# Attention scores as sixteen small products in four quarters of TensorE's array, where four large ones with zero-padded keys stood

## The chip, the cores and the metric

The kernel runs on one core of one Trainium2 chip. The metric is the device time of one execution in microseconds, as the median of several runs. The engines are TensorE (PE; its weight loads are shown as PEld), VectorE (DVE), ScalarE (ACT), GpSimd (POOL) and SyncE (SP), whose queue issues nearly all transfers.

## The reference

Queries, keys and values have the shape (8 batches, 8 heads, 576 tokens, 64). Keys and values are averaged over groups of 8 tokens, so each query sees 72 of them. The attention's output, as a matrix of 4608 tokens by 512, goes through two dense layers with a softplus between.

```python
k_p = k.reshape(B, H, Sp, pool, D).mean(axis=3)        # Sp = 72, pool = 8
v_p = v.reshape(B, H, Sp, pool, D).mean(axis=3)
scores = scale * np.matmul(q, k_p.transpose(0, 1, 3, 2))
scores = scores - np.max(scores, axis=-1, keepdims=True)
attn = np.exp(scores)
attn = attn / (np.sum(attn, axis=-1, keepdims=True) + 1e-09)
attn_out = np.matmul(attn, v_p)
x = attn_out.transpose(0, 2, 1, 3).reshape(B * S, H * D)   # 4608 x 512
h = x @ w_in                                                # 512 x 2048
g = np.maximum(h, 0.0) + np.log1p(np.exp(-np.abs(h)))
out = g @ w_out                                             # 2048 x 512
```

## The kernel before, in words

The 4608 tokens are worked in 18 chunks of 256, each of two tiles of 128 tokens. A batch has 576 tokens, four and a half tiles, so 4 of the 36 tiles hold tokens of two batches: their first 64 tokens see one batch's keys and their last 64 the next one's.

For each tile, PE transposes the queries (`qTp`, L352), ACT copies them out of PSUM (`qT`, L359), PE makes the scores (`sc`, L365), and DVE takes the least of each head's 72 scores (`mn`, L373; the keys carry a negative factor, so the least stands for the greatest) and subtracts it (`E`, L381). In the first three chunks ACT takes the exponential straight from PSUM, with sums (L390). Later one ACT instruction exponentiates a whole chunk. After the sums come transposes of the probabilities (`ptp`, `ltp`), the products with the values (`avp`, L497), and the two dense layers: `h` (L516), the softplus on ACT, and `acc` (L539, L586) or, from chunk 6 on, seven products of quarters in Strassen's manner (`m`, L679), for which DVE forms sums (`sf`, `so`) and which DVE adds up at the end (`o`, `u`, L700). The dense layers use numbers split in a high and a low part, three products each.

The scores before the change: two heads lie one above the other in the 128 partitions of `qT` (64 each). `kbd` holds the scaled keys of such a pair in block form: the first head's 72 keys in partitions 0 to 63 and columns 0 to 71, the second's in partitions 64 to 127 and columns 72 to 143, and zeros elsewhere, which DVE writes once at the start (L180). ACT fills one block (L221) and DVE the other (L223), once per batch. A product of 128 by 128 queries with 144 columns gives two heads' scores of a tile. A tile takes four such products, two into each of two PSUM banks; each bank is a step of its own, with `least` and `less` behind it. A tile of two batches takes eight products, each for 64 tokens. A float32 product is two matmul instructions and two weight loads in the trace.

What sets the order. The program's two parts (the first three chunks with weights being prepared; then the steady part) are each written down as a list of operations with an engine, an estimated cost, predecessors and the buffers they need. A list planner (`Order.run`) plays them against these costs, and every engine's instructions are then issued in the order of its start times. So a changed cost or a merged step moves other instructions too. In the steady part two PSUM banks (kind "bank") serve the transposes, the scores and the value products; two serve `h`; four the outputs. SP's queue runs its transfers in the planned order and waits at each one for what it needs: query, key and value loads, the loads `w<-wi` (a ring for the first layer's weights, L707), and the stores `t<-t` (L654) and loads `w<-t` (L658) of the combined second-layer weights, prepared before chunk 6 by DVE and ACT (L641, L646, L650).

Of the kernel before, what the change touches and what calls it, by code (L numbers as in the profile page):

```python
# [9 lines left out]
F32 = mybir.dt.float32  # L10
# [84 lines left out]
def pooled_attention_softplus_ffn(  # L95
# [79 lines left out]
    kbd = [const.tile([P, HP, 2 * SP], F32, name=f"kbd{i}") for i in range(2)]  # L175
# [40 lines left out]
    def k_block(b, j, ps):  # L216

        pv = ps[j * D:(j + 1) * D, 0:HP * SP].rearrange("p (m j) -> p m j", m=HP)
        o = kbd[b % 2][j * D:(j + 1) * D, :, j * SP:(j + 1) * SP]
        if j == 0:  # L220
            nc.scalar.activation(out=o, in_=pv, func=AF.Copy, scale=SCALE)  # L221
        else:
            nc.vector.tensor_scalar(out=o, in0=pv, scalar1=SCALE, scalar2=None, op0=ALU.mult)  # L223

    def transpose_k(b, kp):
        ps = turn(at_banks, "kT")
        k_transposes(ps, kp)
        for j in range(2):
            k_block(b, j, ps)
# [111 lines left out]
    def new_E(c):  # L341
        e_[c] = one.tile([P, T, H, SP], F32, tag="E", name="E")

    class Tile:
# [16 lines left out]
        def scores(self, i, ps):  # L361
            for m in (2 * i, 2 * i + 1):
                for lo, hi, b in spans(self.first, self.first + P):
                    r = slice(lo - self.first, hi - self.first)
                    nc.tensor.matmul(out=ps[r, (m % 2) * 2 * SP:(m % 2 + 1) * 2 * SP],  # L365
                                     lhsT=self.q[:, m, r], rhs=kbd[b % 2][:, m, :],
                                     start=True, stop=True)

        def least(self, i, ps):

            if i == 0:
                self.mn = two.tile([P, H], F32, tag="mn", name="mn")
            nc.vector.tensor_reduce(out=self.mn[:, 4 * i:4 * i + 4], in_=self.view(ps), axis=AX.X,  # L373
                                    op=ALU.min)

        def view(self, ps):
            return ps[:, 0:4 * SP].rearrange("p (h j) -> p h j", h=4)

        def less(self, i, ps):
            hs = slice(4 * i, 4 * i + 4)  # L380
            nc.vector.tensor_tensor(out=e_[self.c][:, self.t, hs], in0=self.view(ps),  # L381
                                    in1=self.mn[:, hs].unsqueeze(2).to_broadcast([P, 4, SP]),
                                    op=ALU.subtract)

        def exp_sum(self, i, ps):
            if i == 0:
                self.sm = two.tile([P, H], F32, tag="sm", name="sm")
            for j in range(4):
                h = 4 * i + j
                nc.scalar.activation(out=e_[self.c][:, self.t, h], in_=self.view(ps)[:, j],  # L390
                                     func=AF.Exp, scale=-1.0, bias=self.mn[:, h:h + 1],
                                     accum_out=self.sm[:, h:h + 1])
# [62 lines left out]

    def att_tile(c, t):

        x = Tile(c, t)

        def qT():  # L460
            ps = turn(at_banks, "qTp")
            x.qT(ps)
            x.qT_out(ps)

        def scores():
            if c not in e_:
                new_E(c)
            for i in range(2):
                ps = turn(at_banks, "sc")
                x.scores(i, ps)  # L470
                x.least(i, ps)
                x.less(i, ps)

        def norm():
            x.sum()
            x.norm(nc.gpsimd)

        def PT():
            ps = turn(at_banks, "ptp")
            x.PT(ps)  # L480
            x.PT_high(ps)
            x.PT_low(ps)
            ps = turn(at_banks, "ltp")
            x.last(ps)
            x.last_high(ps)
            x.last_low(ps)

        return qT, scores, norm, PT
# [349 lines left out]
    def batch(b):  # L838
# [59 lines left out]
        for i in range(2):  # L898
# [21 lines left out]
        k_done[b] = [op(ACT, act(288), lambda: k_block(b, 0, s_t.tile), [o], [s_t]),  # L920
                     op(DVE, dve1(288) + 0.15, lambda: k_block(b, 1, s_t.tile), [o], [s_t])]
# [22 lines left out]
    def attend(c):  # L944
# [15 lines left out]
        for t, x in enumerate(tiles):  # L960
# [9 lines left out]
            ends = []  # L970
            for i in range(2):
                s = Slot("bank")
                p = op(PE, 0.55 * len(spans(x.first, x.first + P)),
                       lambda x=x, i=i, s=s: x.scores(i, bank(s, "sc")), [o, *keys], [s_qT, s])
# [127 lines left out]
    def keys_values(b):  # L1102
# [8 lines left out]
        for i in range(HP):  # L1111
# [7 lines left out]
        k_ready[b] = [op(ACT, act(288), lambda: k_block(b, 0, s_t.tile), [o], [s_t]),  # L1119
                      op(DVE, dve1(288) + 0.15, lambda: k_block(b, 1, s_t.tile), [o], [s_t])]  # L1120
# [17 lines left out]
    def steady_attention(c):  # L1138
# [10 lines left out]
        for x in tiles:  # L1149
# [6 lines left out]
            last = []  # L1156
            for i in range(2):
                s = Slot("bank")
                p = op(PE, 0.5 if len(sp) == 1 else 0.68,
                       lambda x=x, i=i, s=s: x.scores(i, bank(s, "sc")),  # L1160
# [209 lines left out]
```

## Time and profile before

| | us |
|---|---|
| median of 3 runs | 977.89 |
| the runs | 978.03, 977.89, 975.05 |
| the profiled execution, its own time | 975.02 |
| its span in the trace | 972.9 |
| PE busy in the span | 937.9 (96%) |
| DVE busy | 668.1 (69%) |
| ACT busy | 417.4 (43%) |

The span runs from the first to the last instruction of the trace; 2.1 us of the execution's time lie around it. PE's rows give each matmul a modelled end, so rows of neighbours overlap; what an instruction occupies is read from the starts of the one and the next.

### The profile page before, as it was taken

To read this page: it belongs to the slowest core of one execution; us is meant where nothing else is said; L and a number is where in the kernel's file an instruction comes from. 1 tells how busy PE (TensorE), PEld (TensorE's weight loads), DVE (VectorE), ACT (ScalarE), POOL (GpSimd) and SP (SyncE) were. 2 spreads that over 40 slices of the span, in tenths; PEclk is the share of its full clock that TensorE was granted. 3 is DMA by queue.
4 is the path that set the end of the run, shared out by engine and by line. 5 is a ranking of instruction groups with operands and counts; after the bars stand their busy time and mean duration, and the time that the engine had idled before them with its cause. 6 is when DMAs were issued, how large, how long until landed. Compare 5 with 4: busy or idle time off the path is not lost.

```text
span 972.9 us, 18364 instructions
## 1 busy us (share of the span) xinstructions
PE 937.9 (96%) x7232; PEld 892.0 (92%) x7232; DVE 668.1 (69%) x1468; ACT 417.4 (43%) x826; POOL 119.1 (12%) x149
## 2 busy tenths in 40 slices
PE   5889999999999999999999999999999999999998
PEld 4679898899888999999899999999999999999997
DVE  4799888433699853767788766676767666666654
ACT  4763333433444434435354435443435343444332
POOL 1000001015242100221332320023200000000000
PEclk9999999999999999999999999999999999999999
DMA  9845444133144778886686767487757564755562
GB/s 245 256 170 205 164 152 142 44 102 74 45 156 132 232 256 284 265 230 206 203 234 199 239 192 226 153 242 206 235 152 223 168 216 154 216 174 195 174 217 87
DMA packets 105382, 181.55 MB, mean 187 GB/s; under 512 B 45648, under 2 KB 59984, under 8 KB 105296
## 3 DMA queue, kind: packets, MB, share of 16 engines
q1 hardware_dynamic: 103216, 179.86, 60.0%
q8 instruction: 57, 0.93, 0.4%
q10 hardware_dynamic: 2080, 0.52, 0.3%
q14 instruction: 29, 0.24, 0.1%
HBM read 154.14 MB, written 26.21 MB: 185 GB/s over the span
## 4 chain that ended last, share of the span: by engine, by line
PE 81%; DVE 11%; ACT 4%; issue 2%; DMA 1%; DVEq 0%; ACTq 0%
PE h L516 37%; PE m L679 21%; PE acc L539 6%; PE acc L586 5%; PE sc L365 4%; PE avp L497 3%; DVE sf L605 2%; PE qTp L352 1%; PE ptp L427 1%; DVE d L641 1%; DVE so L615 1%; DVE gl L573 1%; DMA q<-in_q_dram 1%; DVE pm L405 1%; DVE o L700 1%
## 5 line engine op out<-in xcount | busy, mean ns | idle before, releaser
L516 PE MATMUL h<-xh,w 128*128 128x256 f32 x2304 | 421.5, 283 | 2.4 <-DVE w L813 1.2
L516 PEld LDWEIGHTS h<-xh,w 128*128 128x128 f32 x2304 | 355.9, 188 | 6.6 <-DVE w L813 1.7
L516 PE MATMUL h<-xl,w 128*128 128x256 f32 x1152 | 324.1, 281 | 0.0
L567 ACT ACTIVATE g<-h 128x512 f32<-128x512 f32 x240 | 130.5, 596 | 319.4 <-PE h L516 312.7
L516 PEld LDWEIGHTS h<-xl,w 128*128 128x128 f32 x1152 | 216.8, 188 | 0.0
L679 PE MATMUL m<-w,so 128*128 128x256 f32 x1152 | 152.9, 282 | 1.4 <-DVE o L700 1.4
L679 PEld LDWEIGHTS m<-w,so 128*128 128x128 f32 x1152 | 143.7, 188 | 1.8 <-DVE o L700 1.8
L605 DVE TENSOR_TENSOR sf<-g 128x128 f32<-128x128 f32 x192 | 58.5, 305 | 123.1 <-ACT g L567 122.8
L679 PE MATMUL m<-w,g 128*128 128x256 f32 x576 | 113.3, 286 | 0.0
L205 POOL TENSOR_TENSOR kst<-kst 72x512 f32<-72x512 f32 (+1 forms) x48 | 53.5, 1114 | 428.1 <-DMA kst<-in_k_dram 269.4
L573 DVE TENSOR_TENSOR gl<-g 128x512 fp32r<-128x512 f32 x120 | 86.0, 716 | 18.8 <-ACT g L567 18.7
L610 ACT CAST so<-sf 128x512 fp32r<-128x512 f32 x96 | 59.7, 622 | 65.7 <-DVE sf L605 64.5
L679 PEld LDWEIGHTS m<-w,g 128*128 128x128 f32 x576 | 87.9, 188 | 0.0
L679 PE MATMUL m<-w,gl 128*128 128x256 f32 x288 | 81.0, 281 | 0.0
L615 DVE TENSOR_TENSOR so<-sf,so 128x512 fp32r<-128x512 f32 x96 | 72.0, 750 | 7.6 <-ACT so L610 0.9
L373 DVE TENSOR_REDUCE mn<-sc 128x4 f32<-128x288 f32 x72 | 32.4, 455 | 44.0 <-PE sc L365 43.0
L586 PE MATMUL acc<-w,g 128*128 128x512 f32 x192 | 61.1, 399 | 0.0
L539 PE MATMUL acc<-w,g 128*128 128x512 f32 x192 | 60.6, 396 | 0.4 <-ACT g L522 0.4
L522 ACT ACTIVATE g<-h 128x256 fp32r<-128x256 f32 (+1 forms) x96 | 31.9, 383 | 57.8 <-PE h L516 45.8
L679 PEld LDWEIGHTS m<-w,gl 128*128 128x128 f32 x288 | 54.2, 188 | 0.1
L365 PE MATMUL sc<-kbd,qT 128*128 128x144 f32 (+1 forms) x320 | 47.0, 304 | 2.0 <-DVE kbd L223 1.0
L365 PEld LDWEIGHTS sc<-kbd,qT 128*128 128x128 f32 (+1 forms) x320 | 39.8, 187 | 7.5 <-ACT qT L359 3.1
(176 smaller groups left out, 1244.5 us busy)
## 6 DMA issues: line engine op xcount, KB each, us to landing
w<-wi SPq DMA_DIRECT2D x192, 512.0 KB
out_dram<-o SPq DMA_DIRECT2D x36, 256.0 KB
wst<-in_moe_w_in_dram SPq DMA_DIRECT2D x16, 512.0 KB
wst<-in_moe_w_out_dram SPq DMA_DIRECT2D x16, 512.0 KB
wi<-w SPq DMA_DIRECT2D x16, 512.0 KB
t<-t SPq DMA_DIRECT2D x16, 512.0 KB
w<-t SPq DMA_DIRECT2D x32, 256.0 KB
q<-in_q_dram SPq DMA_DIRECT2D x30, 256.0 KB
```

The source lines that it names most:

```text
L205: nc.gpsimd.tensor_tensor(out=out, in0=x, in1=y, op=ALU.add)
L365: nc.tensor.matmul(out=ps[r, (m % 2) * 2 * SP:(m % 2 + 1) * 2 * SP], lhsT=self.q[:, m, r], rhs=kbd[b % 2][:, m, :], start=True, stop=True)
L373: nc.vector.tensor_reduce(out=self.mn[:, 4 * i:4 * i + 4], in_=self.view(ps), axis=AX.X, op=ALU.min)
L516: nc.tensor.matmul(out=ps[:, 0:CT], lhsT=w[:, kc * P:(kc + 1) * P], rhs=x[:, kc], start=first and kc == j == 0, stop=last and kc == KC - 1 ...
L539: nc.tensor.matmul(out=accs[c][t], lhsT=a[:, ts], rhs=w, start=f == 0 and j == 0, stop=f == FC - 1 and j == 2)
L567: nc.scalar.activation(out=g, in_=ps.rearrange("p (k i) -> p k i", k=2), func=AF.Softplus)
L573: nc.vector.tensor_tensor(out=gl, in0=g, in1=gh.bitcast(F32), op=ALU.subtract)
L586: nc.tensor.matmul(out=accs[c][t], lhsT=a[:, k, ts], rhs=w, start=u == 0 and k == 0 and j == 0, stop=u == FP - 1 and k == 1 and j == 2)
L605: nc.vector.tensor_tensor(out=sf[:, o], in0=x, in1=y, op=how)
L610: nc.scalar.copy(out=so[:, 0], in_=ss[c, u])
L615: nc.vector.tensor_tensor(out=so[:, 1], in0=sf, in1=so[:, 0].bitcast(F32), op=ALU.subtract)
L679: nc.tensor.matmul(out=ms[c][n], lhsT=x, rhs=y, start=u == 0 and j == 0 and n in (1, 6, 5, 4), stop=u == FP - 1 and j == 2 and n in (2, 7, ...
```

## The change

The keys are kept without zeros. `kT` holds, for each pair of heads, the 72 scaled keys of the first head in partitions 0 to 63 and of the second in partitions 64 to 127; one ACT instruction writes it from PSUM, and DVE's instruction and the zeroing are gone. A tile's scores are now sixteen products: for each pair of heads `m`, each head `j` of it and each half `i` of the tile's 128 tokens, 64 partitions of queries (64 tokens) against 64 partitions of keys (72 columns). Head `j` picks the upper or lower half of the array's rows and also the PSUM bank; half `i` picks the left or right half of its columns and the upper or lower 64 partitions of the bank. So the four products that follow each other use four different quarters. A tile of two batches takes the same sixteen products, since its border lies at 64 tokens. All sixteen are one planned step that takes both banks at once. `least`, `less` and `exp_sum` then go by `j` (even heads, odd heads) where they went by halves of the heads; their sizes are the same, only the places in the output change.

The planner's cost for the step is 0.7 in place of two steps of 0.5 to 1.1 each, the chain of `least` steps changes slightly, and the stores `t<-t` get a higher priority (`first=1000`). An unused function is removed.

```diff
-    kbd = [const.tile([P, HP, 2 * SP], F32, name=f"kbd{i}") for i in range(2)]
+    kT = [const.tile([P, HP, SP], F32, name=f"kT{i}") for i in range(2)]
...
-        nc.vector.memset(kbd[i], 0.0)
...
-    def k_block(b, j, ps):
-
-        pv = ps[j * D:(j + 1) * D, 0:HP * SP].rearrange("p (m j) -> p m j", m=HP)
-        o = kbd[b % 2][j * D:(j + 1) * D, :, j * SP:(j + 1) * SP]
-        if j == 0:
-            nc.scalar.activation(out=o, in_=pv, func=AF.Copy, scale=SCALE)
-        else:
-            nc.vector.tensor_scalar(out=o, in0=pv, scalar1=SCALE, scalar2=None, op0=ALU.mult)
...
+    def k_scaled(b, ps):
+
+        nc.scalar.activation(out=kT[b % 2], in_=ps[:, 0:HP * SP].rearrange("p (m y) -> p m y", m=HP),
+                             func=AF.Copy, scale=SCALE)
...
-        def scores(self, i, ps):
-            for m in (2 * i, 2 * i + 1):
-                for lo, hi, b in spans(self.first, self.first + P):
-                    r = slice(lo - self.first, hi - self.first)
-                    nc.tensor.matmul(out=ps[r, (m % 2) * 2 * SP:(m % 2 + 1) * 2 * SP],
-                                     lhsT=self.q[:, m, r], rhs=kbd[b % 2][:, m, :],
-                                     start=True, stop=True)
+        def scores(self, pss):
+            for m in range(HP):
+                for j, ps in enumerate(pss):
+                    js = slice(j * D, (j + 1) * D)
+                    for i in range(2):
+                        r = slice(i * P // 2, (i + 1) * P // 2)
+                        b = (self.first + i * P // 2) // S
+                        nc.tensor.matmul(out=ps[r, m * SP:(m + 1) * SP], lhsT=self.q[js, m, r],
+                                         rhs=kT[b % 2][js, m], start=True, stop=True)
...
-        k_ready[b] = [op(ACT, act(288), lambda: k_block(b, 0, s_t.tile), [o], [s_t]),
-                      op(DVE, dve1(288) + 0.15, lambda: k_block(b, 1, s_t.tile), [o], [s_t])]
+        k_ready[b] = [op(ACT, act(288), lambda: k_scaled(b, s_t.tile), [o], [s_t])]
...
-            last = []
-            for i in range(2):
-                s = Slot("bank")
-                p = op(PE, 0.5 if len(sp) == 1 else 0.68,
-                       lambda x=x, i=i, s=s: x.scores(i, bank(s, "sc")),
-                       [o, *parts(sp, k_ready), *last], [s_qT, s], first=EARLY)
-                score_done[c].append(p)
-                last = [op(DVE, 0.46, lambda x=x, i=i, s=s: x.least(i, s.tile), [p], [s, s_mn])]
+            last, ss = [], [Slot("bank"), Slot("bank")]
+            p = op(PE, 0.7, lambda x=x, ss=ss: x.scores([bank(s, "sc") for s in ss]),
+                   [o, *parts(sp, k_ready)], [s_qT, *ss], first=EARLY)
+            score_done[c].append(p)
+            for i, s in enumerate(ss):
+                last = [op(DVE, 0.46, lambda x=x, i=i, s=s: x.least(i, s.tile), [p, *last],
+                           [s, s_mn])]
...
-                o = op(SYNC, 2.0, lambda u=u, part=part: put_t(u, part), [o], [s], lag=2.4)
+                o = op(SYNC, 2.0, lambda u=u, part=part: put_t(u, part), [o], [s], lag=2.4,
+                       first=1000)
```

How the instructions move, at the place where the scores of chunk 8 stand (417 us in the trace), between the last `m` products of chunk 6 and the first `h` products of chunk 7. PE's order before (`w` and `kbd` carry buffer numbers; a row of `sc` or `qTp` counts float32 products; most rows of `h` and `m` between are left out):

```order
L679 MATMUL m<-w_1413,gl 128x256
L352 MATMUL qTp<-ident,q 128x128 x8
L365 MATMUL sc<-kbd_98,qT 128x144 x4
L516 MATMUL h<-xh,w_1510 128x256 x2
...
L516 MATMUL h<-xl,w_1609 128x256
L365 MATMUL sc<-kbd_98,qT 128x144 x4
L516 MATMUL h<-xh,w_1510 128x256 x2
...
L212 MATMUL kT<-ident,kp 128x72 x4
L679 MATMUL m<-w_1704,g 128x256 x2
```

PE's order now, at the same place:

```order
L639 MATMUL m<-w_1477,gl 128x256
L341 MATMUL qTp<-ident,q 128x128 x8
L476 MATMUL h<-xh,w_1574 128x256 x2
...
L476 MATMUL h<-xl,w_1673 128x256
L361 MATMUL sc<-kT_98,qT 64x72 x16
L476 MATMUL h<-xh,w_1574 128x256 x2
...
L639 MATMUL m<-w_1177,so 128x256 x6
L361 MATMUL sc<-kT_98,qT 64x72 x16
L639 MATMUL m<-w_1768,so 128x256 x3
```

Twelve `h` instructions now stand between the query transposes and the first scores, and twelve `h` and twelve `m` (where only twelve `h` stood) between the scores of the first tile and those of the second. On DVE, before, at that place:

```order
L504 TENSOR_TENSOR xl<-avp,xh 128x512 x2
L373 TENSOR_REDUCE mn<-sc 128x4 x2
L381 TENSOR_TENSOR E<-sc,mn 128x288 x2
L373 TENSOR_REDUCE mn<-sc 128x4 x2
L381 TENSOR_TENSOR E<-sc,mn 128x288 x2
L223 TENSOR_SCALAR kbd_97<-kT 64x4x72
L605 TENSOR_TENSOR sf<-g 128x128
```

And now:

```order
L464 TENSOR_TENSOR xl<-avp,xh 128x512 x2
L368 TENSOR_REDUCE mn<-sc 128x4 x2
L374 TENSOR_TENSOR E<-sc,mn 128x4x72 x2
L565 TENSOR_TENSOR sf<-g 128x128
...
L660 TENSOR_TENSOR o<-o,m 128x256 x3
L368 TENSOR_REDUCE mn<-sc 128x4
L565 TENSOR_TENSOR sf<-sf,g 128x128
...
L368 TENSOR_REDUCE mn<-sc 128x4
L374 TENSOR_TENSOR E<-sc,mn 128x4x72 x2
```

The first tile's four instructions still follow each other, but those of the second come later, with sums of chunk 7 and the final additions of chunk 6 ahead of them and among them.

More of the change, by code (lines that the diff above doesn't have):

```diff
@@ L369, in least @@
[L369 to L374, printed above, removed]
-        def view(self, ps):
[L377 to L383, printed above, removed]
@@ new lines, in least, with less @@
+        def least(self, j, ps):
+            if j == 0:
+                self.mn = two.tile([P, 2, HP], F32, tag="mn", name="mn")
+            nc.vector.tensor_reduce(out=self.mn[:, j], in_=self.view(ps), axis=AX.X, op=ALU.min)
+        def view(self, ps):
+            return ps[:, 0:HP * SP].rearrange("p (m y) -> p m y", m=HP)
+        def less(self, j, ps):
+            nc.vector.tensor_tensor(
+                out=e_[self.c][:, self.t].rearrange("p (m j) y -> p j m y", j=2)[:, j],
+                in0=self.view(ps), in1=self.mn[:, j].unsqueeze(2).to_broadcast([P, HP, SP]),
+                op=ALU.subtract)
```

56 lines of the change are left out of this document (11 added, 45 removed).

## The prediction, as it was made

> **What bounds the kernel now.** I read the page first: its busy rows, its slices and the engine shares of the chain that ended last. Then came a table of windows (columns: window, its length, busy us of PE, PEld, DVE, ACT, POOL, then clock, DMA share, GB/s).
>
> ```profile
> PE 937.9 (96%) x7232; PEld 892.0 (92%) x7232; DVE 668.1 (69%) x1468; ACT 417.4 (43%) x826; POOL 119.1 (12%) x149
> PE   5889999999999999999999999999999999999998
> DVE  4799888433699853767788766676767666666654
> PE 81%; DVE 11%; ACT 4%; issue 2%; DMA 1%; DVEq 0%; ACTq 0%
> 0.00:25.00 25.00, 15.24 (x77) 11.06 (x78) 12.36 (x24) 10.58 (x42) 4.22 (x23) 1.00 0.97 244
> 50.00:100.00 50.00, 46.27 (x309) 41.33 (x308) 47.06 (x78) 24.40 (x60) 0.00 (x0) 1.00 0.56 196
> 520.00:700.00 180.00, 176.71 (x1484) 174.37 (x1484) 127.91 (x296) 79.87 (x134) 38.54 (x41) 1.00 0.72 214
> ```
>
> The reader is to see two regimes. From about 70 us on PE is never idle for long (176.71 of 180 us), while DVE has a quarter to spare: a microsecond taken from PE there shortens the run by a microsecond. Before that PE waits for loads, ACT and DVE, and only what lies on the chain counts. Of the 36 tiles, 6 (three chunks) are scored in the first 45 us; 30 are scored later, 27 of one batch and 3 of two (chunks 6, 11 and 15).
>
> **What a tile costs PE now.** Products by shape, all of the run (in the trace a float32 product is two instructions, so 256 instructions are 128 products); then PE's weight loads in order of time around one plain tile, and around the first half of a two-batch tile.
>
> ```profile
> L365 PE MATMUL sc<-kbd,qT 128*128 128x144 f32 x256 | 41.7, 304 | 1.5 <-DVE kbd L223 1.0 <-ACT qT L359 0.2
> L365 PE MATMUL sc<-kbd,qT 128*64 128x144 f32 x64 | 5.9, 305 | 0.5 <-ACT qT L359 0.5
> L365 PEld LDWEIGHTS sc<-kbd,qT 128*128 128x128 f32 x256 | 36.1, 198 | 5.4 <-ACT qT L359 2.1 <-DVE kbd L223 1.2 <-issue 0.8
> L365 PEld LDWEIGHTS sc<-kbd,qT 128*64 128x64 f32 x64 | 3.7, 141 | 2.1 <-ACT qT L359 0.9 <-issue 0.4 <-ACT xh L500 0.2
> 877.07 0.19 PEld L516 LDWEIGHTS h<-xl,w 128*128 128x128 f32 x1
> 877.19 1.04 PEld L365 LDWEIGHTS sc<-kbd,qT 128*128 128x128 f32 x8
> 878.17 0.31 PEld L516 LDWEIGHTS h<-xh,w 128*128 128x128 f32 x2
> 304.84 0.19 PEld L516 LDWEIGHTS h<-xl,w 128*128 128x128 f32 x1
> 305.16 0.44 PEld L365 LDWEIGHTS sc<-kbd,qT 128*64 128x64 f32 x8
> 305.80 0.54 PEld L365 LDWEIGHTS sc<-kbd,qT 128*128 128x128 f32 x4 [0.20 <-issue]
> ```
>
> Plain tile: loads start at 877.19, the next work's at 878.17, and the load before came 0.12 earlier, as usual. So eight instructions take 0.98 us, 0.1225 each: 144 columns.
>
> The two-batch half is the nearest thing to the change. Its eight instructions use 64 of the array's columns each, in turn the left and the right half. From 304.84 to 305.80 is 0.96 us; less the ordinary step of 0.12 it takes 0.84. Eight in a row at 0.1225 would be 0.98, and there is a pause of 0.20 behind (the bracket) and one as long ahead (305.16 less 304.84 less 0.12). What is left, 0.44, fits four steps of 0.1225 (0.49), not eight. So a left and a right half do run at once, and going into the halved array and out again costs 0.84 less 0.49 = 0.35 us. A two-batch tile has two such halves: 1.68 us.
>
> **The change, part by part.**
>
> *Scores.* A tile becomes 32 instructions of 72 columns, four to a group in four different quarters. If all four run at once, a group lasts as long as one: half the columns, half the time, 0.061 us. Its weight load does not bound it: the rows above differ by 57 ns between 128 and 64 columns (198 less 141), so 64 columns cost about 57 ns, just under 61. Eight groups are 0.49; one entry and one exit add 0.35: 0.84 us per tile. Bounds, since no row shows the array cut in rows as well as columns: below, 0.49 (no pause at all); above, 32 instructions with none at once, 1.95 + 0.35 = 2.30. I take 0.84, since the only split seen here overlaps fully. Gain: 27 × (0.98 − 0.84) = 3.8 us, and 3 × (1.68 − 0.84) = 2.5 us.
>
> The trace gives no instruction pace below a pair per 0.1225, so 61 ns per start; the change wants 15. The Trainium skill (TensorE: Matmul & The Clock Gate, "Wait — 56ns, not 53.3ns?") says that start-to-start never drops below about 25 ns however few the columns. By that a group would take 100 ns, a tile 0.80 + 0.35 = 1.15, and the scores' gain would turn into a loss of 3.0 us (27 × 0.17 lost, 3 × 0.53 gained). The pair row here neither confirms nor refutes it, as its mean of 61 ns lies above.
>
> *The wait for the copied queries.* In half of the later chunks the scores stood right behind the query transposes, and PE waited for ACT's copy (columns: us in total, times, longest).
>
> ```profile
> PEld sc L365 <- ACT qT L359: 3.1, 9, 0.5
> 417.04 1.14 PEld L365 LDWEIGHTS sc<-kbd,qT 128*128 128x128 f32 x8 [0.31 <-ACT qT L359]
> 430.38 2.84 PE h L516 x24
> 427.89 2.49 PE m L679 x21
> 875.60 0.95 DVE L373 TENSOR_REDUCE mn<-sc 128x4 f32<-128x288 f32 x2 [1.77 <-PE sc L365]
> 876.46 0.81 DVE L381 TENSOR_TENSOR E<-sc,mn 128x288 f32<-128x288 f32 x2
> DVE mn L373 <- PE sc L365: 43.0, 32, 4.0
> PE m L679 <- DVE o L700: 1.4, 2, 0.7
> ```
>
> Now twelve `h` instructions, half of 2.84 = 1.42 us, stand between, which covers both copies of the two tiles. Gain 3.1 us, of which I count 2.7, since one chunk has the key transposes (which need a bank that ACT frees) there first.
>
> *Both banks at once.* With two banks in all, the second tile's scores wait until DVE has done `mn` and `E` of the first on both: 0.95 + 0.81 = 1.76 us behind the end of the first scores. PE has 1.42 (`h`) + 12/21 × 2.49 = 1.42 (`m`), 2.84 us of other work, and DVE holds these four instructions right behind each other, already standing there (it waited 43.0 us in all for scores). Cost 0 with a cover of 1.1 us; without the cover, each chunk would stall up to 1.76. Queued behind a late `mn` are DVE's sums for `m` and `gl`. Before, the cover was 1.42 and the second tile showed no wait either. The second tile's `mn` and `E` come later now, behind the final additions (`o`), for which PE waited 1.4 us in all; by PE's order nothing needs those banks for two more `h` blocks. I allow −0.5 to +3 us, and take +1.0 for new small stalls of the moved order.
>
> *Keys.* DVE loses 8 instructions and two memsets; ACT's now covers 128 partitions with the same 288 columns, hence the same time.
>
> ```profile
> L223 DVE TENSOR_SCALAR kbd<-kT x8: 460/460/461, 16.0 to 705.5; 64x288 f32<-64x288 f32 x8
> 15.55 0.41 ACT kbd L221
> 15.99 0.47 DVE kbd L223
> 16.50 4.21 PE sc L365 x16
> 26.39 1.18 PE sc L365 x8
> 36.16 0.46 DVE kbd L223
> ```
>
> The last five rows are pieces of the chain of waits in the first 70 us. Two DVE pieces leave it, 0.93 us. The 16 first instructions took 4.21 us, 0.26 each, twice the later pace; four quarters at that pace give 2 × 2 × 0.84 = 3.4, so 0.8 less. Together 1.7, but loads share that stretch (DMA share 0.97) and the order of the first 70 us is mixed anew: bounds −3 (later) to +4 (sooner); I count 1.3 gained. The six later DVE instructions lie off the chain beside PE's work: 0.
>
> *Stores `t<-t`.* They move forward in SP's queue.
>
> ```profile
> SPq L654 <- DVE t L650: 28.2, 7, 8.9
> SPq L707 <- PE h L516: 399.3, 187, 9.5
> ```
>
> SP already stands waiting for DVE at seven of them. What queues behind are loads of later weights, which themselves wait for PE to free their buffers (399.3 us in all), so they hold slack; PE's waits name no such load. 0, and if a load came late, up to the longest wait of 8.9 us once.
>
> **Sum.** 3.8 + 2.5 + 2.7 + 1.3 − 1.0 = 9.3 us less. The profiled execution took 975.0 us (span 972.9 and 2.1 around it), so 965.7 on its own terms. It is at the bottom of the three runs shown, whose median is 2.9 higher; I put the changed kernel's median at 967.
>
> **Rivals.**
>
> 1. *Only two at once (the slower side).* If upper and lower halves of the array's rows take turns, a group takes 0.1225 and a tile 0.98 + 0.35 = 1.33 us. For it: every pair of 64-column instructions in this trace is left against right, none upper against lower. Against it: the quarters share neither partitions of input nor bank. It decides from 0.98, where a plain tile breaks even, which is a group of 0.079. Scores: 27 × 0.35 = 9.5 lost, 3 × 0.35 = 1.1 gained; with the other terms (2.7 + 1.3 − 1.0) 5.4 us slower, about 982 in the median's terms.
>
> 2. *Starts too slow.* Four run at once but cannot be started so fast; halfway between 61 and 122 ns a group takes 92, a tile 1.09. Scores: 27 × 0.11 = 3.0 lost, 1.8 gained; total 1.8 us faster, 975. By the Trainium skill's 25 ns, cited above, the whole change would come to nothing, 976. No overlap at all would be 27 × 1.32 + 3 × 0.62 − 3.0 = 34.5 us slower, 1011.
>
> 3. *New stalls.* The pairing of banks makes PE wait in each of the 14 steady chunks. For it: waits for DVE of up to 2.5 us exist at the probabilities' transposes. Against it: 1.1 us of cover. At 0.7 us each the gain shrinks by 10: no change, 977.
>
> **How the numbers follow.** The forecast 0.66; rival 1 0.11; rival 2 0.10 (without overlap 0.03 of it); rival 3 0.13. The forecast's own range is 959 to 972: the scores' lower bound 0.49 would bring 30 × 0.35 = 10 more, the start's +4 or −3. To hold 8 in 10 I reach up through rivals 2 and 3: 957 to 979. What this kernel's measurement tells from no change is about 0.3%, 2.9 us, so faster is below 975.0: the forecast, half of rival 2's likelier part and a good half of rival 3 make 0.75; slower (rival 1, no overlap, a little of 3) 0.15; the same 0.10.
>
> **What would show it.** In the changed trace the scores' weight loads come in fours at nearly the same time, the fours 0.06 us apart, with a pause of some 0.2 us on either side, and a tile takes 0.84 us from the load ahead to the load behind (rival 1: 1.33, rival 2: 1.09). The row of PE's scores waiting for `qT` is nearly gone; rows of `sc` waiting for DVE's `E` stay under 2 us in all (rival 3: 10). DVE has 10 instructions fewer of `kbd`. The forecast is wrong if a tile takes more than 0.98 us, or if the sum of PE's waits after 100 us grows by more than the scores give back.

## The result and the profile after

The changed kernel takes 961.52 us in the median of 4 runs (958.47 to 962.19), against 976.47 in 4 runs of the kernel before (973.75 to 978.03): a ratio of 0.984, with a 95% interval from 0.981 to 0.988. That is 15 us less; the forecast was a median of 967, range 957 to 979. A second series of the same kernel (below, as a run of its own) gave 959.6 and the same ratio. The profiled executions took 962.13 and 975.02, their spans 960.4 and 972.9.

First the page of the changed kernel, its busy rows and its chain by engine, then a table of windows (window, length, busy us of PE, PEld, DVE, ACT, POOL; clock, DMA share, GB/s).

```profile
PE 925.1 (96%) x8064; PEld 877.0 (91%) x8064; DVE 668.1 (70%) x1458; ACT 414.0 (43%) x824; POOL 120.2 (13%) x149
PE 83%; DVE 11%; ACT 3%; issue 2%; DMA 1%; DVEq 0%; ACTq 0%
```

```profile
0.00:25.00 25.00, 15.15 (x190) 10.50 (x191) 11.48 (x22) 11.33 (x42) 4.21 (x23) 1.00 1.06 253
50.00:100.00 50.00, 46.35 (x297) 41.93 (x296) 45.93 (x71) 19.75 (x46) 0.00 (x0) 0.97 0.53 190
520.00:700.00 180.00, 176.42 (x1637) 173.75 (x1636) 134.02 (x305) 80.71 (x136) 37.07 (x41) 1.00 0.70 217
```

PE's share is still 96%: the same engine bounds the kernel, with 12.8 us less to do (937.9 before). DVE has ten instructions fewer, and its busy time has not moved: two zeroings and eight key copies went, so what stayed takes as much longer.

The scores, as groups by shape, and PE's weight loads around one plain tile late in the run:

```profile
L361 PE MATMUL sc<-kT,qT 64*64 64x72 f32 x1152 | 26.7, 234 | 2.5 <-ACT kT L217 1.8 <-ACT qT L348 0.8
L361 PEld LDWEIGHTS sc<-kT,qT 64*64 64x64 f32 x1152 | 21.7, 138 | 8.6 <-issue 2.2 <-ACT kT L217 2.1 <-ACT qT L348 1.0
```

```profile
866.97 0.78 PEld L639 LDWEIGHTS m<-w,so 128*128 128x128 f32 x6
867.89 0.58 PEld L361 LDWEIGHTS sc<-kT,qT 64*64 64x64 f32 x32
868.55 0.53 PEld L639 LDWEIGHTS m<-w,so 128*128 128x128 f32 x4
```

There are 32 instructions where eight stood. The last of the six loads ahead started at 867.56, one ordinary step of 0.12 later would be 867.68, and the next work loads at 868.55: the tile takes 0.87 us. The single starts of the loads in the trace read 867.886, .893, .900, .906, then 867.941 to .961, 868.003 to .023, 868.066 to .086 and so on to 868.336: four within 20 ns, the fours 62 ns apart (55 for the first step). The products behind them start in the same fours, 7 ns apart: 868.001, .008, .015, .021. Of the 0.87, 0.21 is lost on the way into the quarters, about 0.15 on the way out, and 0.51 is work.

PE's waits after 100 us (total, times, longest) and, last, DVE's for the scores:

```profile
PE ptp L421 <- DVE pm L399: 4.1, 4, 1.3
PE qTp L341 <- DVE xl L464: 3.6, 4, 1.4
PEld sc L361 <- issue: 2.2, 6, 0.4
DVE mn L368 <- PE sc L361: 45.4, 16, 5.9
```

The row of the scores waiting for ACT's copied queries, 3.1 us before, is gone from this stretch, and so is the one of `m` waiting for `o`. The transposes' waits for DVE's `pm` and `xl` changed places (`ptp` for `pm` 2.7 before, for `xl` 2.8 before and 0.4 now; `qTp` 1.8 before) and are 8.1 us in sum, 7.3 before. All in all PE stood idle 13.2 us behind its 151st `h` instruction (92.2 us into the span), against 14.2 before (from 94.7).

Pieces of the chain of waits, in the start:

```profile
15.35 0.42 ACT kT L217
15.81 2.21 PE sc L361 x64
56.68 2.66 PE h L476 x12
61.30 1.44 PE h L476 x12
```

The keys are one piece, and the first two tiles' scores take 2.21 us, not 4.21. Their fours start 0.12 us apart, twice the later step, as the eight instructions of a tile did before (0.24 against 0.12). The trace's record of the clock begins only at 19.5 us (22.6 before), so the clock of 1.00 in the first window says nothing of them. The last two rows are a thing that the prediction did not ask about: the same twelve instructions took 2.66 us and then 1.44. The windows of that stretch, and the same window in the second series' profile of the same kernel, tell why:

```profile
54.40:57.00 2.60, 0.43 (x3) 0.32 (x3) 2.56 (x5) 0.66 (x2) 0.00 (x0) 1.00 0.10 41
57.00:60.40 3.40, 3.40 (x15) 3.13 (x14) 3.10 (x7) 0.66 (x2) 0.00 (x0) 0.51 0.31 123
```

```profile
57.00:60.40 3.40, 3.40 (x25) 3.15 (x24) 3.30 (x7) 0.66 (x2) 0.00 (x0) 1.00 0.27 107
```

PE had waited 2.17 us, and for the next 3.41 us the granted clock was half: 15 products instead of 25. In the other execution the wait was the same and the clock stayed whole. Such a stretch costs some 1.7 us: PE reached its 151st `h` instruction at 92.2 us in the one and at 90.5 in the other.

What differs is where the wait lies against a fixed step. In each of the 14 traces all recorded changes of the clock lie whole multiples of 3.413 us apart, within 3 ns. In the changed kernel's profile one such step runs from 53.63 to 57.04 us and holds the whole wait. In the second series' profile a border of steps, at 55.81, cuts the wait into 1.43 and 0.74 us (first row: the changed kernel's profile; then two of the second series'):

```profile
53.63:57.04 3.41, 1.24 (x11) 1.03 (x10) 3.37 (x7) 0.94 (x4) 0.00 (x0) 1.00 0.10 38
```

```profile
52.40:55.81 3.41, 1.99 (x17) 1.67 (x14) 3.37 (x6) 2.05 (x6) 0.00 (x0) 1.00 0.34 138
55.81:59.22 3.41, 2.67 (x17) 2.47 (x18) 3.27 (x8) 0.66 (x2) 0.00 (x0) 1.00 0.38 154
```

Over all traces, each of the 20 steps at full clock in which PE was busy for less than 0.49 of the time was followed by a half-clock step, none of those with more than 0.71 was, and of 107 in between 12 were (PE's busy time has modelled ends, so these shares are rough). One long wait is not needed: in the kernel before with its stores early (below), two waits, 0.53 and 0.47 us, lie in the step up to 254.66 us, and the next two steps have half the clock.

Each execution lists its mean granted clock, so **time lost to the clock** can be estimated for every run as its time times one less the clock. It leaves out the start, ahead of the clock's first record, and counts 0 to 1.2 us (by profile) at the very end, where the clock is recorded as half and PE is done. Among runs of one kernel, 0.76 us (± 0.10, one standard error, 135 runs) come with each us so lost: a little under one, perhaps as part of it falls where PE waits anyway. The table has means over a kernel's runs; "rest" is the mean less the loss.

| kernel | runs | mean us | lost to the clock | rest |
|---|---|---|---|---|
| before | 53 | 975.7 | 4.7 | 971.0 |
| before, stores early | 11 | 975.5 | 4.7 | 970.8 |
| before, both key blocks by ACT | 11 | 979.9 | 8.8 | 971.1 |
| old products as one step | 10 | 972.1 | 5.4 | 966.7 |
| new products, keys by two engines | 6 | 967.5 | 6.5 | 961.1 |
| the changed order, keys by two engines | 5 | 965.4 | 6.4 | 959.0 |
| changed (both series) | 10 | 960.4 | 2.0 | 958.3 |
| changed, score step planned at 0.87 | 4 | 959.4 | 2.4 | 957.0 |
| changed, DVE planned slower too | 5 | 964.8 | 5.6 | 959.2 |
| changed, stores as before | 10 | 974.3 | 7.8 | 966.5 |
| changed, left against right | 6 | 971.5 | 5.0 | 966.5 |
| changed, upper against lower | 4 | 968.1 | 0.5 | 967.7 |

The single runs of one kernel scatter by 0.9 to 2.3 us (one standard deviation) in "rest", so a mean of five is good to about 1 us. Of the change's 15.3 us, 12.7 are rest and 2.6 are clock.

### The profile page after: what moved, and what is told of

Same layout as the page of the kernel before. It is cut to its first block, busy times and chain, and to the rows that moved or that the text cites. A ratio compares the mean times of both kernels' runs of the same rounds, so it can differ in the third digit from the quotient of the medians.

```text
span 960.4 us, 20024 instructions
## 1 busy us (share of the span) xinstructions
PE 925.1 (96%) x8064; PEld 877.0 (91%) x8064; DVE 668.1 (70%) x1458; ACT 414.0 (43%) x824; POOL 120.2 (13%) x149
## 4 chain that ended last, share of the span: by engine, by line
PE 83%; DVE 11%; ACT 3%; issue 2%; DMA 1%; DVEq 0%; ACTq 0%
PE h L476 39%; PE m L639 22%; PE acc L499 7%; PE acc L546 6%; PE avp L457 4%; PE sc L361 2%; DVE sf L565 2%; PE qTp L341 2%; PE ptp L421 1%; DVE gl L533 1%; DVE so L575 1%; DMA q<-in_q_dram 1%; DVE d L601 1%; ACT g L527 1%; DVE pm L399 1%
## 5 line engine op out<-in xcount | busy, mean ns | idle before, releaser
L639 PE MATMUL m<-w,so 128*128 128x256 f32 x1152 | 155.0, 282 | 0.0
L204 POOL TENSOR_TENSOR kst<-kst 72x512 f32<-72x512 f32 (+1 forms) x48 | 51.3, 1069 | 463.3 <-DMA kst<-in_k_dram 223.0
L533 DVE TENSOR_TENSOR gl<-g 128x512 fp32r<-128x512 f32 x120 | 90.6, 755 | 24.5 <-ACT g L527 24.5
L482 ACT ACTIVATE g<-h 128x256 fp32r<-128x256 f32 x96 | 31.8, 382 | 60.8 <-PE h L476 46.6
L499 PEld LDWEIGHTS acc<-w,g 128*128 128x128 f32 x192 | 34.9, 191 | 7.5 <-ACT g L482 1.1
L546 PEld LDWEIGHTS acc<-w,g 128*128 128x128 f32 x192 | 34.4, 189 | 6.6
```

The lines of the kernel that those rows point to most:

```text
L204: nc.gpsimd.tensor_tensor(out=out, in0=x, in1=y, op=ALU.add)
L482: nc.scalar.activation(out=g, in_=ps[:, 0:CT], func=AF.Softplus)
L499: nc.tensor.matmul(out=accs[c][t], lhsT=a[:, ts], rhs=w, start=f == 0 and j == 0, stop=f == FC - 1 and j == 2)
L533: nc.vector.tensor_tensor(out=gl, in0=g, in1=gh.bitcast(F32), op=ALU.subtract)
L546: nc.tensor.matmul(out=accs[c][t], lhsT=a[:, k, ts], rhs=w, start=u == 0 and k == 0 and j == 0, stop=u == FP - 1 and k == 1 and j == 2)
L639: nc.tensor.matmul(out=ms[c][n], lhsT=x, rhs=y, start=u == 0 and j == 0 and n in (1, 6, 5, 4), stop=u == FP - 1 and j == 2 and n in (2, 7, ...
```

## The experiments

### Which quarters run at once

Three kernels issue a tile's sixteen products in other orders and are otherwise the changed one: pairs of left and right (head by head), pairs of upper and lower (token half by token half), and each quarter's eight instructions in a row. Their loops, in this order:

```diff
-            for m in range(HP):
-                for j, ps in enumerate(pss):
+            for j, ps in enumerate(pss):
+                for m in range(HP):
                     for i in range(2):
```

```diff
-            for m in range(HP):
-                for j, ps in enumerate(pss):
-                    for i in range(2):
+            for i in range(2):
+                for m in range(HP):
+                    for j, ps in enumerate(pss):
```

```diff
-            for m in range(HP):
-                for j, ps in enumerate(pss):
-                    for i in range(2):
+            for j, ps in enumerate(pss):
+                for i in range(2):
+                    for m in range(HP):
```

> The same sixteen products per tile, in another order: neighbours differ only in the left or right half of the array's columns, so only two quarters can be busy at once. Every engine's order is otherwise that of the changed kernel. Theory (the gain of the scores comes from four quarters at once): a pair every 0.0625 us, a tile 16 x 0.0625 + 0.37 = 1.37 us in place of 0.87, thus 30 x 0.50 = 15 us more than the changed kernel's 961.5, and 1 to 3 more at the start: 977 to 980. Rival (the gain comes from the moved order of the other instructions, the products hardly count): within 4 us of 961.5.

> The same sixteen products, neighbours differing only in the upper or lower half of the array's rows (and so in the bank). Theory (rows overlap as columns do): as left against right, 977 to 980, a pair every 0.0625 us. Rival (upper and lower halves overlap only when the columns differ too): one product after the other, a tile 32 x 0.0625 + 0.37 = 2.37 us, 45 us more: 1004 to 1010.

> The same sixteen products, four of one quarter in a row before the next quarter. Theory: nothing overlaps except where the quarter changes, a tile 2.2 to 2.4 us, 40 to 46 us more than the changed kernel: 1001 to 1012. Rival (products of a later quarter are pulled ahead of those that wait): close to 962.

Measured: left against right 971.06 us (ratio to before 0.995, 0.992 to 0.997), upper against lower 967.76 (0.991, 0.988 to 0.995), one quarter after the other 998.71 in one run. PE's weight loads around a tile in each, in this order:

```profile
874.42 0.78 PEld L639 LDWEIGHTS m<-w,so 128*128 128x128 f32 x6
875.34 0.88 PEld L361 LDWEIGHTS sc<-kT,qT 64*64 64x64 f32 x32
876.30 0.77 PEld L639 LDWEIGHTS m<-w,so 128*128 128x128 f32 x6
```

```profile
872.17 0.88 PEld L361 LDWEIGHTS sc<-kT,qT 64*64 64x64 f32 x32
873.13 0.77 PEld L639 LDWEIGHTS m<-w,so 128*128 128x128 f32 x6
```

```profile
898.95 1.48 PEld L361 LDWEIGHTS sc<-kT,qT 64*64 64x64 f32 x32
900.51 0.30 PEld L476 LDWEIGHTS h<-xh,w 128*128 128x128 f32 x2
```

From the first score load to the load behind, a tile takes 0.96 us in both kernels of pairs and 1.56 in the third, against 0.66 in the changed kernel. The rows of the array are cut as well as its columns: in the second kernel's trace upper and lower products start in pairs too, 872.172 with .178, 872.286 with .293, 872.348 with .355, so an upper and a lower half overlap as fully as a left and a right one. Rival 1 falls.

The sizes were missed. With pairs only, 16 steps of 62 ns would be 1.00 us, 0.50 more than the changed tile's eight, where 0.30 was measured. In the third, 32 steps would be 2.00 and came to 1.41 (1.56 less the exit of 0.15). The single starts of its products show how: 898.948, 899.061, then every 62 ns to 899.249, and from there often two at a time, 899.249 with 899.255, 899.368 with 899.374, 899.430 with 899.436. So the second quarter starts 0.31 us after the first, whose own eight starts take 0.48 from first to last: its first product starts ahead of the first quarter's last ones, which stand before it in the program. The same shows later, where the trace names the product: the one at 899.743 signals the first bank as done, so it is the second quarter's last, and the third quarter's first, which stands behind it in the program, had started at 899.561. In strict order, with each quarter's first load beside the last one of the quarter before, the last load would start 28 steps, 1.75 us, behind the first; it started 1.35 behind. It looks as if PE took, from the next few products, those whose quarter is free.

The Trainium skill (TensorE: Matmul & The Clock Gate, "Part 3: Packing small matmuls — row/col tiling") says that products start and end strictly in program order. By that the last pair could start no sooner than 14 steps of 62 ns, 0.875 us, behind the first, and the next work 0.21 later, at 1.09; it came at 0.96, and the trace decides against the rule, for starts at least.

In the table the rest of the two kernels of pairs is 8.2 and 9.4 us above the changed kernel's. Thirty steady tiles by 0.30 are 9.0. The tile accounts for the whole difference, and the 3 us between these two kernels are clock (5.0 and 0.5 lost).

### The plan without the new products

The kernel before, with its eight products of a tile as one step that takes both banks, planned at 0.7 as in the change, and with the stores early:

```diff
-            for i in range(2):
-                s = Slot("bank")
-                p = op(PE, 0.5 if len(sp) == 1 else 0.68,
-                       lambda x=x, i=i, s=s: x.scores(i, bank(s, "sc")), ...
+            last, ss = [], [Slot("bank"), Slot("bank")]
+            p = op(PE, 0.7, lambda x=x, ss=ss: x.scores([bank(s, "sc") for s in ss]), ...
```

> The kernel before with only the planning of the change: the old products of 144 columns with zeros in the keys, but as one step of both banks at the new cost of 0.7, and the earlier stores. Theory (products and order both count): a plain tile 0.98 us against 0.87 and a two-batch tile about 1.35, thus 27 x 0.11 + 3 x 0.48 = 4.4 us more than the changed kernel, and 1 to 2 more for the keys at the start: 966 to 969, and 6 to 9 us less than before. Rival (the products make nearly all of the gain): 973 or more.

Measured: 971.86 us (0.996, 0.994 to 0.998), between the two forecasts.

```profile
L365 PE MATMUL sc<-kbd,qT 128*128 128x144 f32 x256 | 37.7, 294 | 1.0 <-DVE kbd L223 1.0
L365 PE MATMUL sc<-kbd,qT 128*64 128x144 f32 x64 | 4.8, 292 | 1.5 <-DVE E L381 1.5
```

The products are the old ones, and no row of them waits for `qT` any more. The rest is 4.3 us below the kernel before. The forecast has two terms for that: the wait for the queries (2.7), and one way into and out of the halved array less in each of three two-batch tiles (3 × 0.35 = 1.05); 3.75 together. This run does not separate them, and it has the early stores, without which the new order loses time (below). The second row's wait, 1.5 us once for DVE's `E`, is the largest stall of rival 3's kind; `h` and `kT` wait 0.5 and 0.3 us for it besides.

Next the new products on top, in the same order on every engine, with each key block still written by its own engine, ACT or DVE, into the keys without zeros:

```diff
+        o = kT[b % 2][j * D:(j + 1) * D]
+        if j == 0:
+            nc.scalar.activation(out=o, in_=pv, func=AF.Copy, scale=SCALE)
+        else:
+            nc.vector.tensor_scalar(out=o, in0=pv, scalar1=SCALE, scalar2=None, op0=ALU.mult)
```

> The changed kernel, but the keys without zeros are written in two halves by ACT and DVE as before. Every engine's order comes out as in the run with the old products in one step (e4), so against that run only the products differ (and two memsets); against the changed kernel the writer of the keys and the order of some transposes and value products differ. Theory: the products give 27 x 0.115 + 3 x 0.46 = 4.5 us after the start and about 1 in it: 5.5 us under e4's 971.9, so 966 to 967, and the other 5 of the changed kernel's gain over e4 come from the keys' writer through the order. Rival (the products give all of the 10 us between e4 and the changed kernel, the writer nothing): 961 to 962.5.

Measured: 967.34 us (0.992, 0.988 to 0.995). That is 4.5 less than the kernel just above by the medians and 5.6 by the rest, good to some 2 us. The thirty later tiles alone would give 27 × (0.98 − 0.87) + 3 × (1.68 − 0.35 − 0.87) = 4.4, and the six in the start add to it. So, within that error, the products bring what their own time says. Two of PE's waits here do not stand in the changed kernel's list:

```profile
PE ltp L441 <- DVE kT L222: 1.6, 1, 1.6
PE sc L365 <- DVE E L378: 1.6, 1, 1.6
```

### Who writes the keys

What is left from there to the changed kernel is one ACT instruction where ACT and DVE wrote, and the order that the planner makes of it. Two kernels split it. The first keeps the changed kernel's order and lets ACT and DVE write; the second is the kernel before with both key blocks written by ACT, in two instructions.

```diff
-        k_ready[b] = [op(ACT, act(288), lambda: k_scaled(b, s_t.tile), [o], [s_t])]
+        k_ready[b] = [op(ACT, act(288), lambda: [k_block(b, j, s_t.tile) for j in range(2)], [o], [s_t])]
```

In the second, the planner's two steps also become one ACT step of twice the cost, so that kernel's order moves as well:

```diff
-        if j == 0:
-            nc.scalar.activation(out=o, in_=pv, func=AF.Copy, scale=SCALE)
-        else:
-            nc.vector.tensor_scalar(out=o, in0=pv, scalar1=SCALE, scalar2=None, op0=ALU.mult)
+        nc.scalar.activation(out=o, in_=pv, func=AF.Copy, scale=SCALE)
```

> The changed kernel in its own order on every engine, but the keys are written half by ACT and half by an added DVE instruction at that place. Theory (the changed kernel gains over the run with two writers by the order that one writer allows in the first 60 us): 960 to 963. Rival (DVE, which does its work in order, holds the keys' bank and PE waits for it): 964 to 968, with PE waiting for DVE's kT row.

> The kernel before with both blocks of the keys with zeros written by ACT. Theory (fewer hand-overs of the keys' bank between engines help at the start): 1 to 4 us faster than before. Rival (the old order gains nothing from it, since its losses lie at the scores): within 1.5 us of before or slower.

Measured: 965.25 us (0.990, 0.986 to 0.993) for the first, 978.6 (1.005, 1.002 to 1.007) for the second, which was expected faster and is slower. The first run's time is that of its rival, but not by the rival's mechanism, PE's wait for DVE's keys.

From the first, in its profile, which is the slowest of five runs: DVE's key row and what it waited for, PE's timeline at its longest late wait, and the windows around it.

```profile
L222 DVE TENSOR_SCALAR kT<-kT x8: 460/460/461, 15.0 to 692.9; 64x288 f32<-64x288 f32 x8
  ACT kT L220: 6.5, 5
```

```profile
701.11 0.65 PE L425 MATMUL ptp<-ident,pm 128*128 128x128 f32 x4 [2.30 <-DVE pm L403]
```

```profile
698.90:702.30 3.40, 1.06 (x8) 0.85 (x9) 3.37 (x6) 1.53 (x3) 2.48 (x2) 1.00 0.77 273
702.30:705.70 3.40, 3.40 (x18) 3.40 (x18) 3.27 (x9) 0.97 (x3) 0.00 (x0) 0.51 0.01 4
705.70:709.10 3.40, 3.40 (x31) 3.40 (x30) 0.71 (x2) 0.00 (x0) 0.00 (x0) 0.99 0.15 29
```

DVE goes through its list in the planned order, so its key copy, which waits five times for ACT's, 6.5 us in all, holds up what is queued behind it. Of that PE feels little directly: its scores wait 0.3 us for DVE's half of the keys. It feels a late `pm`: 2.30 us at 698.8, six microseconds behind the last key copy (692.9). From that copy to the `pm` DVE's pieces follow each other without a pause; the copy is 0.46 us of them, and what else made `pm` late was not separated. And PE pays again, since the next 3.41 us have half the clock: 18 products where the window behind has 31. The table puts it in one number: the rest is 959.0, within the scatter of the changed kernel's 958.3, but 6.4 us are lost to the clock, not 2.0. That its five half-clock stretches go back to the key copy is not shown; three of them lie before 61 us, where waits for loads and DVE are mixed.

The second kernel says the same from the other side: its rest is the kernel before's to a tenth, 971.1, and its 4.2 us more are all clock (8.8 lost). Taking the copy from DVE was worth nothing in the old form, where ACT then does two instructions; why its order bunches PE's waits so is open.

### The stores

The changed kernel with the stores at their old priority, and the kernel before with the stores early:

```diff
-                o = op(SYNC, 2.0, lambda u=u, part=part: put_t(u, part), [o], [s], lag=2.4,
-                       first=1000)
+                o = op(SYNC, 2.0, lambda u=u, part=part: put_t(u, part), [o], [s], lag=2.4)
```

> The changed kernel without the higher priority of the stores of the combined weights. PE's order stays as it is, only SP's changes. Theory (the stores lie beside PE's work): no change, 960 to 963.5. Rival (late stores would hold up loads): 3 us or more slower, with PE waiting for loads after 370 us.

> The kernel before with nothing but the higher priority of the stores of the combined weights. PE's order is that of before, SP's moves at 40 rows. Theory (the priority only undoes a stall that the new order would bring, and the old order has none): within 3 us of the kernel before. Rival (the early stores are worth something in any order): 5 us or more faster.

Measured: 973.78 us without the priority (0.999, 0.997 to 1.001), and 975.38 with it in the kernel before (1.000, 0.998 to 1.002). So the priority does nothing to the old order, and without it the new order loses the whole gain, where no change was expected; nor did PE wait for late loads, as the rival had it. It loses most of it in one place. From the changed kernel without the priority: PE's wait, pieces of the chain, ACT's timeline there, and windows of PE alone (length, busy us; clock, DMA share, GB/s).

```profile
PE m L639 <- ACT so L570: 7.2, 1, 7.2
```

```profile
370.83 2.86 PE h L476 x24
...
374.09 6.78 DMA t<-t
380.86 0.02 issue
380.89 0.63 ACT so L570
381.51 0.04 issue
381.56 3.87 PE m L639 x15
385.42 3.96 PE h L476 x24
```

```profile
380.89 0.62 ACT L570 CAST so<-sf 128x512 fp32r<-128x512 f32 x1 [6.09 <-DMA t<-t]
```

```profile
374.00:381.00 7.00, 0.38 (x4) 0.75 0.97 305
381.00:384.00 3.00, 2.44 (x10) 0.50 0.89 243
384.00:387.00 3.00, 3.00 (x16) 0.50 0.13 50
```

The last two stores are issued at 374.09 and take 6.78 us to land, beside loads that keep the transfer engines 97% busy. Both tiles, `t` and `so`, carry `tag="S"` in a pool of two buffers, so the two stores hold both, and the first `so` of the Strassen chunks has to wait for one. PE stands 7.2 us, and its clock is half until 387.8: 24 `h` instructions take 3.96 us, not 2.86. In the table it lies 8.2 us of rest and 5.8 of clock above the changed kernel (some of the half-clock time falls in the wait itself). In the changed kernel the last store is out long before:

```profile
339.65 0.32 SPq L614 DMA_DIRECT2D t<-t  x1
```

In the kernel before, the last store was as late (377.94), but the one ahead of it had left at 363.20, so a buffer was free: the first `so` ran at 373.75 and had waited for DVE alone.

### The planner's costs

The changed kernel once more; with the score step planned at its measured 0.87; and with DVE's costs raised to its measured ones as well.

```diff
-            p = op(PE, 0.7, lambda x=x, ss=ss: ...
+            p = op(PE, 0.87, lambda x=x, ss=ss: ...
```

```diff
-        return 0.14 + 0.00106 * n
+        return 0.14 + 0.0012 * n
...
-            o = op(DVE, 1.14, lambda: sums(c, u), [g], [s_g, s_f], first=HURRY)
+            o = op(DVE, 1.24, lambda: sums(c, u), [g], [s_g, s_f], first=HURRY)
```

> The changed kernel itself once more, for a second trace of it and its spread. 960 to 963; the first 80 us of the new trace within 2 us of the old one's.

> The changed kernel with the scores' step planned at 0.87, what it measured, in place of 0.7. PE's order moves at 30-odd places, nearly all in the first 200 us. Theory (the steady part is ruled by PE's work, the start by ACT, DVE and loads): within 2 us of the changed kernel. Rival (the changed kernel's start is a lucky order): 3 us or more slower, all of it in the first 90 us.

> The changed kernel with the planner's costs as the traces measure them: scores 0.87, DVE's subtractions of 512 columns 0.75 in place of 0.68, its sums 1.24 in place of 1.14. If PE's remaining 12 us of waits after 100 us come from DVE being later than planned, a third of them go: 955 to 958. If they are the places of the chunk's border where nothing else is at hand: 959 to 963.

Measured: 959.6 (0.984, 0.981 to 0.987), 958.94 (0.983, 0.980 to 0.987) and 965.58 (0.989, 0.985 to 0.993). The first two can't be told apart. The third was expected to be the best and is some 5 us worse, and again the rest is not: 959.2. Its windows around a wait of 2.12 us of `ptp` for DVE's `xl`:

```profile
598.40:601.80 3.40, 1.28 (x12) 1.11 (x11) 3.37 (x6) 1.08 (x2) 1.40 (x2) 1.00 0.72 218
601.80:605.20 3.40, 3.40 (x19) 3.38 (x17) 3.15 (x9) 1.47 (x3) 0.00 (x0) 0.51 0.28 107
```

With truer costs PE was idle as long in sum (13.0 us behind the 151st `h` instruction), but its longest wait there is 2.12 us, where the changed kernel's is 1.38. That is one of this profile's three half-clock stretches; the other two lie in the start (42 and 59 us), and why its start loses them is open. No kernel tried is clearly faster than the changed one.

## Why the prediction was right, and where not

It forecast a gain of 9.3 us in the profile's terms, and 15.3 came (means of the runs). Its steps in turn:

| step | forecast | measured, and by what |
|---|---|---|
| tile of scores | 0.84 us | 0.87, trace |
| new products, later tiles, without the merged step | 5.25 | 5.6 ± 2 of rest, start included; 4.4 by the tile |
| merged step (3 × 0.35) and the wait for queries | 3.75 | 4.3 of rest |
| new stalls | −1.0 | within the rows above |
| keys | 1.3 | 2.8 of rest, writer and order together |
| stores | 0 | 0 against the kernel before |
| clock | no term | 2.6 |

**Scores.** All four quarters run at once, as the split of left and right let one expect; the pace of a group, 61 ns forecast and 62 measured, and the price of entry and exit, 0.35 and 0.36, were read rightly from the half of a two-batch tile. Rival 1 would have had 1.33 us for a tile and rival 2 1.09. Starts 7 ns apart also show that the rule of 25 ns does not hold between products of different quarters. The prediction said that its pair row neither confirms nor refutes the rule; that was a misreading, since the single starts behind that row, in the profile of before, are 7 ns apart as well (305.338 with .345, 305.460 with .467).

**The wait for queries** went as said, and with it the order: twelve `h` instructions do stand between.

**New stalls**, the term of −1.0 and rival 3, did not come. Single ones did (1.0 us of `h` for `E`, once), but as many went, and PE's idle time fell from 14.2 to 13.2 us. The cover that the prediction worked out held.

**Keys** was the mis-sized term. It counted two DVE pieces off the chain in the start and put the six later ones at 0, because PE had other work. Nearly so in time: with DVE writing in the same order the rest rises by 0.7, and the other 2.1 of the 2.8 are the order. But with DVE writing the kernel loses 4.4 us more to the clock, for which the step had no reason. The term also held the first two tiles' scores, put at 3.4 us for 4.21. They took 2.21: the step had doubled the price of entry and exit with the pace, and counted it for each tile.

**The clock** is the step that was missing. The sum treated a microsecond of PE's waiting as a microsecond. The profile of before had a window that says otherwise, and it was not read:

```profile
30.00:40.00 10.00, 8.62 (x58) 7.13 (x55) 8.63 (x22) 7.78 (x36) 0.00 (x0) 0.83 1.05 322
```

A clock of 0.83 over 10 us is one stretch of 3.4 at half, and ahead of it lies a step with three waits, the longest 0.73 us, 1.36 in all. Idle time that bunches in one step of 3.41 us is followed, or not, by 3.4 us at half rate, so it costs its own length and up to 1.7 more. The kernel before loses 4.7 us so in the mean, the changed one 2.0. No experiment moved the borders of the steps, so that they decide is read from the traces alone.

**Stores.** The result 0 holds against the kernel before, but the reason was wrong: what queues behind them in SP's queue is not what matters. They hold buffers that `so` needs, and the new order reaches `so` with both taken unless they go early. That part of the change is worth 14 us in the new order (973.78 against 959.6), and nothing in the old.

**The range.** Nearly all errors point the same way, so the measured 961.5 lies low in it. The lower end of the forecast's own range, 959, does not follow from the prediction's bounds, either: 10 us off 967 is 957, before the start's +4.

## What to carry to other kernels

Small float32 products that use different quarters of the array, with their outputs in different partitions or banks, do run four at once, measured here for 64 by 64 by 72; count some 0.36 us for going in and out, and let neighbours in the program use different quarters. When orders of the same work are compared, read the mean granted clock of every run beside its time: two orders with equal work and equal idle time differ here by 3.6 us of clock, and the half-clock stretches came where PE was idle for 0.29 or more of one step of 3.41 us, in one wait or in several, and always where it was idle for more than 0.51. So look for places where PE's idle time bunches, not at its sum over the run. A store that looks idle in its queue still holds its buffer: ask who takes that buffer next.

## What the hardware showed that was not expected

- Products of different quarters do not start in program order: with the quarters one after the other, the second began 0.31 us behind the first, whose own eight starts took 0.48.
- Loads of different quarters start 7 ns apart, 32 of them in 0.45 us.
- After waits of 2.17, 2.12 and 2.30 us, PE's clock was half for 3.41 us each time, and after the same 2.17 us in another execution of the same kernel, where a border of the 3.413 us steps cut the wait in two, it was not. After 7.2 us it was half for about 10 us. The Trainium skill (TensorE: Matmul & The Clock Gate, "Why this matters for your kernels") warns of waits above about 3 us; here shorter ones did it. The Trainium skill's same page has a watching window of 3.4 us that runs freely ("What's actually happening"), and the length of 3.41 us, the steps on which all changes lie and the difference between two executions agree with that.
